# Clustered attention: the row of maxima copied directly, two int64 staging buffers, and new slots for every preparation step

## The chip, the cores and the metric

One Trainium2 chip, one of its cores. The metric is device time in microseconds of one execution; lower is better. The core has five engines that run side by side, each in the order of its own program: TensorE (PE in the rows; PEld is its weight load), VectorE (DVE), ScalarE (ACT), GpSimd (POOL), and SyncE (SP), whose sequencer issues all the transfers of this kernel.

## What is computed

Clustered attention, followed by two mixture layers whose code the change does not touch. With 4 batches, 8 heads, 768 positions and a head dimension of 64:

```python
q_assign = np.argmax(np.einsum('bhsd,hcd->bhsc', q_n, c_n), axis=-1)
k_assign = np.argmax(np.einsum('bhsd,hcd->bhsc', k_n, c_n), axis=-1)
mask = q_assign[:, :, :, None] == k_assign[:, :, None, :]
scores = scale * np.matmul(q, k.transpose(0, 1, 3, 2))
scores = np.where(mask, scores, -1000000000.0)
scores = scores - np.max(scores, axis=-1, keepdims=True)
attn = np.exp(scores)
attn = attn / (np.sum(attn, axis=-1, keepdims=True) + 1e-09)
return np.matmul(attn, v).astype(np.float32)
```

The result goes through `g = h * cos(h)` with `h = x @ w_in`, where `w_in` and `w_out` are 64-bit floats that the kernel receives as int64 and converts itself, and then through a soft mixture of eight experts.

## The kernel before

The attention works on 16 pairs of heads. For each pair there is a stack `st` in SBUF (three of them, used in turn), with the high and low parts of q and k, 32 rows that encode the cluster mask, and on partition 96 one row that holds, for each query, its maximum with the sign turned. The score matmuls (L399, L400) read this stack, so that the maximum is subtracted by the matmul itself, and ScalarE's exponential (L403) needs no bias. A pair has 12 units `u`: two chunks of 384 queries by six tiles of 128 keys, with a score for each of the two heads. After every second unit the matmuls with v follow (`av`, tile `o`, L412), and GpSimd adds up the exponentials (`ps`, L417 and L420).

While pair j is scored, the next pairs are made ready. For pair j+1 there are 24 maxima matmuls (`smax`, tile `sm`, L364), each emptied by a reduction of VectorE (`mc`, L366). `smax_fin` gathers the maxima of one chunk, and `smax_row` turns them by a transpose (L379) into a tile `mrow` of 6 partitions by 128 (L381) and brings them to partition 96 of the stack. For pair j+2 q and k are transposed (`prep_T`), split into high and low parts (`prep_hi`, `prep_lo`: qlo and klo on VectorE, L275) and copied to the stack; `prep_cl`, `prep_ct`, `prep_mx`, `prep_eq`, `prep_eqt`, `prep_mask` and `prep_rows` make the mask rows. Beside that two blocks of 128 by 512 weights are converted per pair: `conv_load` fetches the int64 words into the tile `w64`, `conv_do` has eight steps (0, 1, 3, 4, 5 and 6 on VectorE, 2 and 7 on ScalarE). In this text cvo0 to cvo7 are the steps of the first block of a pair (w_out), cvi0 to cvi7 those of the second (w_in).

The order of all this is written out by hand in the tables `POS` and `FIRST` (L521 to L544). A pair has 48 slots, four to a unit: before the first score, between the scores, after the second score, and after `av`. `at4(g, q, f)` puts a step into slot q of the pair that begins at unit g. `FIRST` holds the slots of the first pair, which runs with less prepared. The program is emitted in that order, so the slot of a step sets its place on every engine. Transfers that need an engine's result are put off by a number of slots (`defer`, `tick`), and SyncE issues them in that order; a transfer that has to wait holds all the later ones.

Nearly all matmuls of the preparation share three PSUM banks in turn (`mbank`), so a matmul can start only when the bank that was used three matmuls earlier has been emptied.

The row of maxima goes to partition 96 in two transfers, through a DRAM tile:

```python
defer(DL, out=mds[i, qc], in_=mrow.bitcast(F32))
defer(DL + 6, out=st[96:97, Q1:Q1 + 2, QW * qc:QW * qc + QW].bitcast(F32),
      in_=mds[i, qc].rearrange("(o h t) p -> o h (t p)", h=2, o=1))
```

Of the kernel before, what the change touches and what calls it, by code (L numbers as in the profile page):

```python
# [8 lines left out]
F32 = mybir.dt.float32  # L9
F32R = mybir.dt.float32r  # L10
BF16 = mybir.dt.bfloat16
I32 = mybir.dt.int32
# [7 lines left out]
P = 128  # L20
# [6 lines left out]
def clustered_attention_then_soft_moe(  # L27
# [20 lines left out]
    NPAIR = B * NP  # L48
    KT = S // P
    QW = S // 2  # L50
# [10 lines left out]
    dram = ctx.enter_context(tc.tile_pool(name="dram", bufs=1, space=DRAM))  # L61
# [6 lines left out]
    def mbank(nm, shape=(P, 512), dt=F32):  # L68
        mcnt[0] += 1
        return psum.tile(list(shape), dt, tag=f"m{mcnt[0] % ring[0]}", name=nm)  # L70
# [8 lines left out]
    mask = const.tile([P, 2], F32, name="mask")  # L79
    vm = const.tile([P, NPAIR], F32, name="vm")  # L80
# [4 lines left out]
    sums = [dram.tile([H, S], F32, name=f"sums{b}") for b in range(B)]  # L85
    recs = [dram.tile([H, S], F32, name=f"recs{b}") for b in range(B)]
    wod = dram.tile([DF, DM], F32, name="wod")
    mds = {(i, c): dram.tile([6, P], F32, name=f"mds{i}_{c}") for i in range(NPAIR) for c in range(2)}

    wc = [wbig.tile([P, 2, DT, 512], F32R, tag="wbig", name=f"wc{f}") for f in range(NF)]  # L90

# [58 lines left out]
    with ExitStack() as a:  # L150
        at_p = a.enter_context(tc.tile_pool(name="at", bufs=3))
        two = a.enter_context(tc.tile_pool(name="a2", bufs=2))
# [4 lines left out]
        Q1, Q2, K1, K2 = 0, 2, 4, 6  # L157
        T = {}
        late = []
        DL = 3  # L160

        def defer(n, **kw):
            late.append([n, kw])
# [212 lines left out]
        def smax_row(i, qc):  # L376
            s, st = T[i], stacks[i % 3]
            g = mbank(f"mrow{i}_{qc}")
            PE.transpose(g[0:6, 0:P], s["m6", qc], ident)  # L379
            mrow = two.tile([6, P], F32R, tag="mrow", name=f"mrow_{i}_{qc}", bufs=1)  # L380
            DVE.tensor_scalar(out=mrow, in0=g[0:6, 0:P], scalar1=-BIG / 2, scalar2=-1.0, op0=ALU.max, op1=ALU.mult)  # L381
            defer(DL, out=mds[i, qc], in_=mrow.bitcast(F32))
            defer(DL + 6, out=st[96:97, Q1:Q1 + 2, QW * qc:QW * qc + QW].bitcast(F32),
                  in_=mds[i, qc].rearrange("(o h t) p -> o h (t p)", h=2, o=1))

        def smax_rowpe(i, qc):
            s, st = T[i], stacks[i % 3]
# [59 lines left out]

        def conv_load(n):
            w, r, c = conv[n]
            st = two.tile([P, 1024], I32, tag="w64", name=f"w64_{n}", bufs=1)  # L450
            src = w_in if w == "i" else w_out
            SP.dma_start(out=st, in_=src[r * P:(r + 1) * P, c * 512:(c + 1) * 512].bitcast(I32))
            T["c", n] = st
# [61 lines left out]
        def at(g, pos, f, *args):  # L515
            fill.setdefault((g, pos), []).append((f, args))

        def at4(g, q, f, *args):
            at(g + q // 4, q % 4, f, *args)

        POS = {  # L521
            "T": [3, 7, 0, 1, 7, 12, 17, 23],
            "c": [12, 16],
            "m": [16, 20, 25, 28],
            "rows": [42, 35, 42, 36],
            "ld": 16,
            "cv": [[4, 4, 4, 8, 9, 12, 16, 17], [28, 29, 30, 35, 37, 42, 42, 45]],
            "wp": [23, 34, 40],
            "sm": [0, 5, 6, 7, 10, 10, 15, 17, 18, 26, 26, 27, 20, 21, 21, 32, 34, 36, 36, 40, 41, 43, 45, 46],
            "fin": [1, 4, 30, 35],  # L530
            "vm": [6, 28, 19],
        }
        FIRST = {
            "eqt": 7,
            "mask": 8,
            "rows": [9, 12, 12, 10],
            "cv": [3, 6, 8, 11, 15],
            "ld": 9,
            "wp": [21, 26, 36],
            "sm0": [2, 2, 5, 5, 6, 7, 8, 12, 15],  # L540
            "sm1": [13, 15, 16, 21, 22, 24, 24, 25, 26, 26, 28, 29, 17, 29, 31, 33, 34, 38, 40, 41, 42, 42, 44, 45],
            "fin0": [15, 19],
            "fin1": [33, 35],
        }  # L544

        def place_conv(n, g):
            pos = POS["cv"][n % 2]
            for k, x in enumerate(pos):
                at4(g, x, conv_do, n, k)
            if n + 1 < len(conv):  # L550
                at(g + pos[5] // 4 + 1, 0, conv_load, n + 1)
            if conv[n][0] == "o":
                r = conv[n][1]
                for x, f in zip(POS["wp"], (wphi_T, wphi_mm, wphi_sum)):
                    at4(g, x, f, r)

        for n in range(1, len(conv)):
            place_conv(n, 12 * (n // 2))
# [42 lines left out]
        for j in range(NPAIR):  # L601
            g = 12 * j
            f = POS["fin"]
            if j:
                at(g - 8, 0, load_v, j)
                at4(g, f[0], smax_fin, j, 1, True)
                at4(g, f[1], smax_row, j, 1)
            if j > 1:
                at4(g - 12, f[2], smax_fin, j, 0, True)
                at4(g - 12, f[3], smax_row, j, 0)  # L610
            at4(g, POS["vm"][0], prep_vm, j)
            at4(g, POS["vm"][1], prep_vm2, j)
            if j < NPAIR - 1:
                at4(g + 12, POS["vm"][2], sumq, j)
            if j % NP == NP - 1 and j < NPAIR - 1:
                at(g + 20, 2, recip0, j // NP)
                at(g + 23, 3, recip, j // NP)
# [19 lines left out]
        def flush():  # L637
            while late:
                tick()

        conv_load(0)
        ACT.activation(out=cn, in_=cn, func=AF.Exp, scale=-1.0)
        consts2()
# [46 lines left out]
        for x in range(3, 8):  # L690
            at4(0, FIRST["cv"][x - 3], conv_do, 0, x)
        at4(0, FIRST["ld"], conv_load, 1)
        for x, f in zip(FIRST["wp"], (wphi_T, wphi_mm, wphi_sum)):
            at4(0, x, f, 0)
        pend = []
        for g in range(GE):
            i, u = divmod(g, NU)
# [58 lines left out]
    with ExitStack() as m:  # L756
# [299 lines left out]
        for h in range(2):  # L1056
            x = slice(256 * h, 256 * h + 256)
            DVE.scalar_tensor_tensor(out=acc[:, x], in0=acc[:, x], scalar=cr, in1=ap[h], op0=ALU.mult, op1=ALU.add)
            g = psum.tile([P, 512], F32, tag="s", name=f"acct{h}", bufs=3)[:, 0:256]
# [164 lines left out]
```

## Time and profile before

| | us |
|---|---|
| runs of the kernel | 957.63, 959.75, 960.16 |
| median | 959.75 |
| profiled execution | 960.29 |
| its span, first to last instruction | 958.4 |
| mean granted clock of TensorE | 0.989 |

The page has the busy time of each engine, the idle time before groups of instructions and what ended it, and the chain of work that ended last. A matmul's end is modelled: consecutive score matmuls start 0.18 us apart, though each is shown with 0.34 us. So what a wait costs is best read from the starts, and the idle time that the trace gives is about 0.16 us less. A stretch from about 32 to 503 us is the attention; the two mixture layers follow.

### The profile page before, as it was taken

To read this page: it belongs to the slowest core of one execution; us is meant where nothing else is said; L and a number is where in the kernel's file an instruction comes from. 1 tells how busy PE (TensorE), PEld (TensorE's weight loads), DVE (VectorE), ACT (ScalarE), POOL (GpSimd) and SP (SyncE) were. 2 spreads that over 40 slices of the span, in tenths; PEclk is the share of its full clock that TensorE was granted. 3 is DMA by queue.
4 is the path that set the end of the run, shared out by engine and by line. 5 is a ranking of instruction groups with operands and counts; after the bars stand their busy time and mean duration, and the time that the engine had idled before them with its cause. 6 is when DMAs were issued, how large, how long until landed. Compare 5 with 4: busy or idle time off the path is not lost.

```text
span 958.4 us, 16925 instructions
## 1 busy us (share of the span) xinstructions
PE 904.9 (94%) x5994; PEld 622.8 (65%) x5994; DVE 716.2 (75%) x1459; ACT 674.5 (70%) x1420; POOL 459.3 (48%) x342
## 2 busy tenths in 40 slices
PE   5798999999999999999999999999999999999995
PEld 3465666666666666656656777777777777677543
DVE  6778888988888888879786777777777777775402
ACT  4657888777887778867664677767776777676423
POOL 3437877788777878776862222222222222220000
PEclk9889999999999999999999999999999999999998
DMA  8966667776668766676231043304331111117899
GB/s 173 211 149 157 162 175 196 192 197 155 166 176 213 191 172 166 174 186 166 89 95 54 24 132 117 125 25 132 119 123 36 33 37 31 45 26 295 333 360 326
DMA packets 132515, 142.18 MB, mean 148 GB/s; under 512 B 58408, under 2 KB 105808, under 8 KB 132432
## 3 DMA queue, kind: packets, MB, share of 16 engines
q1 hardware_dynamic: 132432, 141.11, 53.2%
q8 instruction: 47, 0.77, 0.3%
q14 instruction: 36, 0.29, 0.1%
HBM read 86.27 MB, written 17.06 MB: 108 GB/s over the span
## 4 chain that ended last, share of the span: by engine, by line
PE 68%; DVE 11%; ACT 9%; DMA 7%; issue 2%; SPq 2%; POOL 0%; ACTq 0%; POOLq 0%
PE h L138 21%; PE o L412 12%; PE sm L364 6%; PE s L399 6%; PE s L400 5%; PE gt L784 3%; DVE mc L366 3%; DMA mds<-mrow 3%; PE lp L810 2%; PE accp L893 2%; DVE qlo L275 2%; ACT L772 2%; DMA st<-mds 2%; PE he L1101 1%; ACT L848 1%
## 5 line engine op out<-in xcount | busy, mean ns | idle before, releaser
L138 PE MATMUL h<-wc,xhi 128*128 128x512 f32 x768 | 249.6, 406 | 6.7 <-DVE gg L777 6.5
L420 POOL TENSOR_TENSOR ps<-ps,a 128x768 f32<-128x768 f32 x120 | 235.3, 1961 | 37.9 <-ACT a L403 18.2
L366 DVE TENSOR_REDUCE mc<-sm 128x1 f32<-128x384 f32 x384 | 199.1, 547 | 30.3 <-PE sm L364 27.9
L403 ACT ACTIVATE a<-s 128x384 f32<-128x384 f32 x384 | 175.8, 491 | 26.2 <-PE s L400 20.4
L138 PEld LDWEIGHTS h<-wc,xhi 128*128 128x128 f32 x768 | 137.3, 189 | 56.9 <-DVE kk L147 15.9
L138 PE MATMUL h<-wc,xlo 128*128 128x512 f32 x384 | 151.7, 395 | 0.0
L399 PE MATMUL s<-st 97*128 97x384 f32 x384 | 141.8, 369 | 7.3 <-DMA st<-mds 6.9
L412 PE MATMUL o<-a,vt 128*64 128x384 f32 x768 | 147.7, 506 | 0.0
L364 PE MATMUL sm<-st 96*128 96x384 f32 x384 | 135.8, 385 | 10.1 <-DVE mc L366 6.1
L400 PE MATMUL s<-st 128*128 128x384 f32 x384 | 130.5, 340 | 0.0
L364 PEld LDWEIGHTS sm<-st 96*128 96x128 f32 x384 | 72.4, 194 | 50.4 <-DVE mc L366 17.5
L777 DVE SCALAR_TENSOR_TENSOR gg<-kk,h 128x512 f32<-128x512 f32 x96 | 66.0, 687 | 50.6 <-ACT kk L774 47.8
L772 ACT ACTIVATE kk<-kk 128x512 f32<-128x512 f32 x96 | 60.6, 631 | 42.0 <-DVE kk L147 41.7
L399 PEld LDWEIGHTS s<-st 97*128 97x128 f32 x384 | 73.1, 190 | 23.1 <-issue 11.1
L412 PEld LDWEIGHTS o<-a,vt 128*64 128x64 f32 x768 | 47.2, 137 | 57.6 <-issue 57.3
L109 POOL TENSOR_TENSOR xn<-xn,rc 128x512 f32<-128x512 f32 x24 | 31.3, 1304 | 109.0 <-DMA rc<-recs 109.0
L138 PEld LDWEIGHTS h<-wc,xlo 128*128 128x128 f32 x384 | 72.2, 188 | 17.0
L400 PEld LDWEIGHTS s<-st 128*128 128x128 f32 x384 | 73.4, 191 | 0.0
L417 POOL TENSOR_TENSOR ps<-a,a 128x768 f32<-128x768 f32 x30 | 54.8, 1827 | 37.5 <-ACT a L403 33.7
L113 POOL TENSOR_TENSOR xn<-xn,rc 128x512 f32<-128x512 f32 x24 | 32.0, 1332 | 84.0 <-DVE rc L111 78.9
L121 POOL TENSOR_TENSOR xlo<-xn,xhi 128x512 fp32r<-128x512 f32 x24 | 36.5, 1522 | 67.5 <-DVE xhi L120 66.0
L147 DVE SCALAR_TENSOR_TENSOR kk<-kk,h 128x512 f32<-128x512 f32 x96 | 66.0, 688 | 3.3
(218 smaller groups left out, 1530.0 us busy)
## 6 DMA issues: line engine op xcount, KB each, us to landing
w<-in_moe_w_dram SPq DMA_DIRECT2D x8, 2048.0 KB
wh<-in_moe_w_dram SPq DMA_DIRECT2D x26, 512.0 KB
st<-qhi SPq DMA_DIRECT2D x32, 384.0 KB
st<-khi SPq DMA_DIRECT2D x64, 192.0 KB
w<-in_moe_w_out_dram SPq DMA_DIRECT2D x16, 512.0 KB
w<-in_moe_w_in_dram SPq DMA_DIRECT2D x16, 512.0 KB
qt<-in_q_dram SPq DMA_DIRECT2D x32, 192.0 KB
kt<-in_k_dram SPq DMA_DIRECT2D x32, 192.0 KB
```

Of the source, the lines that this page charges most:

```text
L138: PE.matmul(h, lhsT=x[:, d, :], rhs=wc[f][:, w, d, :], start=(n == 0), stop=(n == 3 * DT - 1))
L147: DVE.scalar_tensor_tensor(out=a, in0=a, scalar=-TWO_PI, in1=h, op0=ALU.mult, op1=ALU.add)
L364: PE.matmul(m[:, 0:QW], lhsT=st[0:96, Q1 + h, qt * P:(qt + 1) * P], rhs=st[0:96, K1 + h, half * QW:(half + 1) * QW], start=True, stop=True)
L366: DVE.tensor_reduce(out=s["mc"][:, col:col + 1], in_=m[:, 0:QW], op=ALU.max, axis=AX.X)
L399: PE.matmul(x[:, 0:QW], lhsT=st[0:97, K1 + h, ks], rhs=st[0:97, Q1 + h, qs], start=True, stop=False)
L400: PE.matmul(x[:, 0:QW], lhsT=st[:, K2 + h, ks], rhs=st[:, Q2 + h, qs], start=False, stop=True)
L403: ACT.activation(out=T[i][u][:, h, :], in_=x[:, 0:QW], func=AF.Exp, scale=scale)
L412: PE.matmul(s["o"][64 * h:64 * h + 64, 0:QW], lhsT=s["v"][:, h, kt, :], rhs=t[:, h, :], start=(kt == 0), stop=(kt == KT - 1))
L417: (DVE if i == NPAIR - 1 else POOL).tensor_tensor(out=ps, in0=s[u - 1], in1=t, op=ALU.add)
L420: (DVE if i == NPAIR - 1 else POOL).tensor_tensor(out=ps, in0=ps, in1=t, op=ALU.add)
L772: ACT.activation(out=r, in_=r, func=AF.Sin, scale=0.5)
L777: DVE.scalar_tensor_tensor(out=R["g", t][:, f * 512:(f + 1) * 512], in0=r, scalar=0.5, in1=h, op0=ALU.subtract, op1=ALU.mult)
```

## The change

The row of maxima goes from `mrow` straight to partition 96, in two transfers of three partitions each, one for each head, and the DRAM tiles `mds` are gone. The staging tile `w64` gets two buffers instead of one, and the load of the next block has slots of its own (`cl`) instead of following step 5 of the block before. All the numbers of `POS` and `FIRST` but a few are new.

```diff
-    mds = {(i, c): dram.tile([6, P], F32, name=f"mds{i}_{c}") for i in range(NPAIR) for c in range(2)}
...
-            defer(DL, out=mds[i, qc], in_=mrow.bitcast(F32))
-            defer(DL + 6, out=st[96:97, Q1:Q1 + 2, QW * qc:QW * qc + QW].bitcast(F32),
-                  in_=mds[i, qc].rearrange("(o h t) p -> o h (t p)", h=2, o=1))
+            for h in range(2):
+                defer(DL, out=st[96:97, Q1 + h, QW * qc:QW * qc + QW].bitcast(F32).rearrange("o (t p) -> o t p", p=P),
+                      in_=mrow[3 * h:3 * h + 3].bitcast(F32))
...
-            st = two.tile([P, 1024], I32, tag="w64", name=f"w64_{n}", bufs=1)
+            st = two.tile([P, 1024], I32, tag="w64", name=f"w64_{n}")
...
-            "rows": [42, 35, 42, 36],
+            "rows": [35, 35, 38, 43],
...
-            "fin": [1, 4, 30, 35],
-            "vm": [6, 28, 19],
+            "fin": [3, 6, 34, 36],
+            "vm": [24, 30, 11],
+            "cl": [1, 41],
...
-                at(g + pos[5] // 4 + 1, 0, conv_load, n + 1)
+                at4(g, POS["cl"][n % 2], conv_load, n + 1)
```

On SyncE, the transfers at the end of a pair: before, the row goes to DRAM and comes back (the second waits for the landing of the first, DMAHW6), and the load of the next int64 block waits for VectorE and ScalarE to have read the buffer. The names in brackets are the counters that an instruction waits for.

```order
L170 DMA st_153<-klo_1432 64x768 [waits DMAHW3_49,DVE_49]
L170 DMA st_153<-klo_1432 64x768 [waits DMAHW4_49]
L170 DMA xnum_81<-num_0_1463 128x384 [waits DMAHW5_49,Activation_49]
L170 DMA mds_0_100<-mrow_0_1526 6x128 [waits DMAHW6_49,DVE_49]
L170 DMA st_152<-mds_0_100 1x2x384 [waits DMAHW7_49,DMAHW6_49]
L452 DMA w_6_1581<-in_moe_w_out_dram 128x1024 [waits DMAHW0_49,DVE_49,Activation_49]
```

The same place with the change:

```order
L169 DMA xnum_81<-num_0_1044 128x384 [waits DMAHW2_49,Activation_49]
L169 DMA st_120<-klo_1046 64x768 [waits DMAHW3_49,DVE_49]
L169 DMA st_120<-klo_1046 64x768 [waits DMAHW4_49]
L169 DMA st_122<-mrow_0_1119 1x3x128 [waits DMAHW5_49,DVE_49]
L169 DMA st_122<-mrow_0_1119 1x3x128 [waits DMAHW6_49]
L451 DMA w_4_1152<-in_moe_w_out_dram 128x1024 [waits DMAHW7_49]
```

Two transfers of half a row have taken the place of the two hops, and each waits for the row on VectorE but for no landing of the other hop.

On VectorE, from the fifth step of the first conversion block to the first maxima of the second half, before (qlo is the low part of q; t and val belong to the conversion):

```order
L476 SCALAR_TENSOR_TENSOR t_4_1257<-w_4_1198,t_4_1257 128x512
L275 TENSOR_TENSOR qlo_1326<-qT_1251,qhi_1294 128x768
L366 TENSOR_REDUCE mc_1223<-sm_6_1347 128x1
L478 TENSOR_TENSOR val_1258<-val_1258,t_4_1257 128x512
L307 TENSOR_REDUCE amx_1359<-e_1357 128x24
L366 TENSOR_REDUCE mc_1223<-sm_7_1376 128x1
L366 TENSOR_REDUCE mc_1223<-sm_8_1383 128x1
```

With the change, from the two maxima of slot 10 to sm_15:

```order
L365 TENSOR_REDUCE mc_1191<-sm_2_1277 128x1
L365 TENSOR_REDUCE mc_1191<-sm_13_1280 128x1
L473 TENSOR_SCALAR t_4_1217<-w_4_1152 128x512
L274 TENSOR_TENSOR qlo_1307<-qT_1220,qhi_1270 128x768
L365 TENSOR_REDUCE mc_1191<-sm_14_1314 128x1
L475 SCALAR_TENSOR_TENSOR t_4_1217<-w_4_1152,t_4_1217 128x512
L365 TENSOR_REDUCE mc_1191<-sm_3_1323 128x1
L477 TENSOR_TENSOR val_1218<-val_1218,t_4_1217 128x512
L365 TENSOR_REDUCE mc_1191<-sm_4_1344 128x1
L306 TENSOR_REDUCE amx_1359<-e_1333 128x24
L311 TENSOR_TENSOR eq_1363<-e_1333,amx_1359 128x384
L365 TENSOR_REDUCE mc_1191<-sm_5_1370 128x1
```

The conversion's steps 5 and 6 have moved behind qlo, and eq ahead of sm_5.

On TensorE, the end of that stretch with the change (s are scores, wt the transposes of a converted block):

```order
L398 MATMUL s_5_0_1365<-st_122 128x384
L399 MATMUL s_5_0_1365<-st_122 128x384
L363 MATMUL sm_5_1370<-st_120 128x384
L398 MATMUL s_5_1_1373<-st_122 128x384
L399 MATMUL s_5_1_1373<-st_122 128x384
L363 MATMUL sm_6_1377<-st_120 128x384
L489 MATMUL wt_1380<-ident,val_1218 128x128 x4
L363 MATMUL sm_15_1387<-st_120 128x384
```

The maxima sm_5, sm_6 and the transposes wt take the three banks, and sm_15 is the next to need sm_5's; before, sm_12 to sm_14 stood at this place.

## Rows read from the trace of the kernel before

**Rows 1.** Busy time by stretch: length, then each engine, granted clock, DMA share.

```profile
99.00:128.00 29.00, 28.24 (x174) 18.18 (x174) 25.39 (x45) 23.28 (x52) 22.94 (x17) 1.00 0.70 182
```

**Rows 2.** Timeline of TensorE, first scores of pairs 1 and 13: start, duration, work.

```profile
74.26 0.34 PE L399 MATMUL s<-st 97*128 97x384 f32 x1
...
427.32 0.45 PE L399 MATMUL s<-st 97*128 97x384 f32 x1 [1.81 <-DMA st<-mds]
```

**Rows 3.** Waits of the whole span: total us, times, longest.

```profile
DVE t L466 <- DMA w<-in_moe_w_out_dram: 28.3, 14, 3.7
...
PEld s L399 <- DMA st<-mds: 9.9, 12, 2.1
...
PE sm L364 <- DVE mc L366: 6.1, 9, 1.5
```

**Rows 4.** Chain of waits, 244 to 252 us, and the matmul before its last piece.

```profile
244.36 0.28 DVE mrow L381
...
244.84 4.29 DMA mds<-mrow
...
249.14 1.82 DMA st<-mds
...
249.71 0.41 PE L364 MATMUL sm<-st 96*128 96x384 f32 x1
251.01 0.44 PE L399 MATMUL s<-st 97*128 97x384 f32 x1 [0.89 <-DMA st<-mds]
```

**Rows 5.** Chain of waits: eight o matmuls behind 427 us, and eight usual ones.

```profile
428.77 2.76 PE o L412 x8
434.92 1.44 PE o L412 x8
```

**Rows 6.** Timeline of TensorE, 231 to 235 us.

```profile
231.16 0.34 PE L400 MATMUL s<-st 128*128 128x384 f32 x1
232.22 0.44 PE L364 MATMUL sm<-st 96*128 96x384 f32 x1 [0.72 <-DVE mc L366]
...
234.03 0.85 PE L432 MATMUL sum<-ps,ones 128*32 128x384 f32 x8
```

**Rows 7.** Timeline of TensorE: the waits in the first pair and at its end.

```profile
44.81 0.45 PE L364 MATMUL sm<-st 96*128 96x384 f32 x1 [1.52 <-DVE mc L366]
...
73.98 0.44 PE L364 MATMUL sm<-st 96*128 96x384 f32 x1 [1.45 <-ACT st L335]
```

**Rows 8.** Timeline of VectorE: qlo and eq without and with a neighbour.

```profile
47.73 0.94 DVE L275 TENSOR_TENSOR qlo<-qT,qhi 128x768 fp32r<-128x768 f32 x1
...
56.34 0.55 DVE L312 TENSOR_TENSOR eq<-e,amx 128x384 bf16<-128x384 f32 x1
...
229.27 2.43 DVE L275 TENSOR_TENSOR qlo<-qT,qhi 128x768 fp32r<-128x768 f32 x1
...
234.07 1.62 DVE L312 TENSOR_TENSOR eq<-e,amx 128x384 bf16<-128x384 f32 x1
```

**Rows 9.** Timeline of GpSimd: the addition that runs when the second qlo starts.

```profile
229.05 1.83 POOL L417 TENSOR_TENSOR ps<-a,a 128x768 f32<-128x768 f32 x1
```

**Rows 10.** Timeline of TensorE: first and last matmul of a stretch in pair 7.

```profile
256.50 0.51 PE L364 MATMUL sm<-st 96*128 96x384 f32 x2
...
265.78 0.42 PE L399 MATMUL s<-st 97*128 97x384 f32 x1
```

**Rows 11.** Groups of VectorE: busy, mean ns of one, idle before.

```profile
L366 DVE TENSOR_REDUCE mc<-sm 128x1 f32<-128x384 f32 x384 | 199.1, 547 | 30.3 <-PE sm L364 27.9
L275 DVE TENSOR_TENSOR qlo<-qT,qhi 128x768 fp32r<-128x768 f32 x15 | 27.3, 1818 | 0.2 <-ACT qhi L258 0.2
L312 DVE TENSOR_TENSOR eq<-e,amx 128x384 bf16<-128x384 f32 x16 | 22.9, 1429 | 0.1
L472 DVE SCALAR_TENSOR_TENSOR val<-val,t 128x512 f32<-128x512 f32 x32 | 21.7, 677 | 0.0
```

**Rows 12.** Busy time and granted clock (after POOL) by stretch in the first pair.

```profile
46.00:54.00 8.00, 7.43 (x32) 3.74 (x29) 3.60 (x5) 2.08 (x5) 3.13 (x2) 0.57 1.09 232
```

More of the change, by code (lines that the diff above doesn't have):

```diff
@@ L521, in clustered_attention_then_soft_moe @@
         POS = {
-            "T": [3, 7, 0, 1, 7, 12, 17, 23],
-            "c": [12, 16],
-            "m": [16, 20, 25, 28],
-            "rows": [42, 35, 42, 36],
[L526 to L529, printed above, removed]
-            "fin": [1, 4, 30, 35],
-            "vm": [6, 28, 19],
+            "T": [3, 8, 0, 3, 9, 12, 16, 28],
+            "c": [11, 15],
+            "m": [19, 20, 26, 28],
+            "rows": [35, 35, 38, 43],
+            "ld": 8,
+            "cv": [[3, 5, 5, 10, 11, 14, 15, 23], [29, 29, 29, 36, 39, 42, 43, 45]],
+            "wp": [23, 29, 41],
+            "sm": [0, 6, 10, 14, 17, 21, 22, 25, 26, 26, 28, 34, 1, 10, 13, 24, 33, 34, 36, 37, 38, 40, 44, 44],
+            "fin": [3, 6, 34, 36],
+            "vm": [24, 30, 11],
+            "cl": [1, 41],
         }
         FIRST = {
[L534 to L543, printed above, removed]
+            "eqt": 2,
+            "mask": 2,
+            "rows": [12, 10, 9, 10],
+            "cv": [0, 2, 7, 13, 23],
+            "ld": 11,
+            "wp": [25, 27, 44],
+            "sm0": [0, 1, 3, 5, 7, 7, 10, 16, 19],
+            "sm1": [12, 14, 14, 16, 19, 21, 23, 23, 29, 30, 31, 34, 18, 20, 21, 26, 27, 33, 38, 40, 42, 42, 42, 44],
+            "fin0": [19, 21],
+            "fin1": [36, 38],
         }
```

## The prediction

> **What bounds the kernel now.** I read the page first, then the busy time by stretch, the waits, the chain around one pair's start, and the timelines of TensorE, VectorE and GpSimd there. The profiled execution took 960.29 us, its span 958.4. The change touches the attention stage alone, from about 32 to 503 us. There TensorE is busy for 28.2 of 29 us in an undisturbed stretch, while VectorE has 25.4, ScalarE 23.3 and GpSimd 22.9 [rows 1]. So TensorE sets the pace, and a change here is worth what it takes from TensorE's idle time, no more. What is idle shows in the pairs' starts: pair 1 starts at 74.26 us and pair 13 at 427.32 [rows 2], so twelve pairs take 353.1 us, 29.4 each. The two waits that are costed below take 9.9 and 5.5 us of them, 1.3 a pair, so about 28.1 is the floor that the matmuls and the small waits set. The prize over twelve pairs is some 15 us, and a little more in the first pair and the thirteenth.
>
> The waits name it [rows 3]. TensorE's weight loads wait 9.9 us in 12 places for st<-mds, which is the row of maxima coming back from DRAM. Its matmuls wait 6.1 us in 9 places for a reduction of VectorE (L366), which must empty one of three PSUM banks. VectorE in turn stands 28.3 us in 14 places waiting for the int64 weights w. The last is no loss by itself: VectorE is not the bound and these waits lie at a pair's opening, where few reductions are due.
>
> **The row of maxima.** In the chain from 244 to 251 us the row is computed at 244.36, the copy to DRAM is issued at 244.84 and takes 4.29 us, the copy back takes 1.82 more, and the first score matmul of the next pair starts at 251.01 [rows 4]. The matmul before it stands at 249.71, so without the wait it would have started at 249.97 and 1.04 us were lost. The change drops the first copy and issues two copies of half a row instead, so the count of transfers stays at four per pair and SyncE's queue gets no longer. It also stops holding SyncE until the first copy has landed. The row is now made one slot later and behind one more reduction of 0.5 us, so it is ready about 4.7 us before the pair's start, where it was 5.3. What one direct copy of 1.5 KB takes, no row shows. The nearest short one is the copy back, 1.82 us. The long one of the same chain is the copy to DRAM, 4.29. The first copy was issued 0.2 us after the row, and I allow 0.5 for issuing two (an estimate); the second half then lands 2.5 or 5.0 us after the row. I take the short value: in the old order the copy to DRAM stands right behind klo's two copies and num's, with khi's four shortly before; in the new one khi's four stand 19 slots ahead of the row, klo's two 8 slots ahead, and the load of w behind it. So the wait goes: **-9.9 us**. With the long value 0.3 us at 14 starts would come back, +4.2. The other row of a pair, due in the middle, is issued behind the new load of q and k but has 15 slots until it is needed, about 8.8 us at 0.585 us a slot (28.1 over 48), so I cost that move at nothing.
>
> One start cost more. At 427.32 TensorE had been idle for 1.81 us by the gap column, and the eight o matmuls behind it took 2.76 us where eight normally take 1.44 [rows 2, 5]. If that wait goes, so does the slow stretch: **-1.3 us**.
>
> **The reduction that frees a bank.** At 232.22 a maximum matmul (L364) starts 1.06 us after its predecessor at 231.16, where 0.18 is usual [rows 6]; 0.88 is lost, of which the gap column shows 0.72. The 6.1 us in 9 places [rows 3] hold 1.52 from the opening [rows 7] and a short one of 0.2; what is left is 4.4 in seven pairs, with 0.16 more each 5.5. The cause stands on VectorE: qlo took 2.43 us in this pair and 0.94 where GpSimd had nothing to do [rows 8]. In the slow case a ps addition of GpSimd of 1.83 us had begun 0.22 us earlier [rows 9], and qlo ended 0.82 us after that addition. The late bank was that of sm_6, whose reduction stood right behind qlo. In the new order sm_14 stands there, and its bank is wanted again by sm_4 after much the same matmuls. But one conversion step of 0.68 now stands behind qlo instead of ahead of it [rows 11], and the sums, 0.85 on TensorE [rows 6], come before sm_14 instead of behind: about 1.5 us more room where 0.88 were lost. **-5.5 us** from the old place.
>
> The same price has to be asked of the new order. The tight place there is sm_15, which needs the bank that the reduction of sm_5 frees. From the two maxima in slot 10 to sm_15 TensorE runs two groups of o, six scores, cl, the sums, ct, wt and seven maxima. The same set with one more maximum lies between 256.50 and 265.78 in a pair without that stall [rows 10]: 9.28 us, so 9.1. VectorE must do in it three steps of the conversion at 0.68, six reductions at 0.52 (busy time by count), amx, a reduction like them, qlo and eq [rows 11]. Without the last two that is 5.7 us, and the first reduction starts when its matmul of 0.44 ends [rows 6], so 6.1. With the means 1.82 and 1.43 it is 9.4, which exceeds 9.1 by 0.3. With 0.94 and 0.55, the unhindered values [rows 8], nothing is lost; with 2.43 and 1.62 it is 10.2 and 1.1 are lost. I take the mean, since GpSimd is as full as before: 13 pairs by 0.3, **+4 us** (0 to +14.3).
>
> The Trainium skill (SBUF — State Buffer, "Who interferes with whom") says that a VectorE instruction with two SBUF inputs and a GpSimd instruction that reads SBUF exclude each other for the whole instruction. By that rule the worst qlo would be 0.94 + 1.83 = 2.8 us and the top of this term about 19 instead of 14.3; the trace agrees with the order of things, its longest being 2.5.
>
> **The second staging buffer.** It takes away the 28.3 us of VectorE. I cost it at nothing on TensorE's path, as said, though it is why VectorE enters the tight stretch without backlog. If its load came late after all, VectorE would again stand 2 us there (28.3 in 14 places), with the same small effect as now. The five additions of prep_vm move from slot 6 to 24 on GpSimd and their reader vm2 from 28 to 30; GpSimd has 6 us free in 29 [rows 1], so I cost this at nothing.
>
> **The prepared mask rows.** At 73.98 the first maximum of the next pair waits 1.45 us for ScalarE's st rows (L335) [rows 7]. In the table two of the four row steps move from slot 42 to 35 and 38, and the one that the first maximum needs is done by 39 even in the pair that runs four slots late: **-1.6 us**.
>
> **The opening (first pair).** Before, TensorE waits 1.52 us at 44.81, and the granted clock is 0.57 of full speed from 46 to 54 us [rows 7, 12], most of it at the lower of the two levels (1.2 of 2.4 GHz); 8 us at 0.43 less are 3.4 us of work lost. The new first table puts all four row steps of VectorE at one place, earlier, and the maxima of pair 1 right behind ScalarE's last row step. It can lose all of the 4.9 or add another wait like the 1.45. I take 0 (-4.9 to +1.5).
>
> Sum: -9.9 - 1.3 - 5.5 + 4 - 1.6 = -14.3, so 946.0 for the profiled execution's 960.29. Its time stands 0.5 above the median of the runs, 959.75, so the forecast is **945.5 us**. About 0.3% (2.9 us) is what a measurement of this kernel can tell from no change. The later stages (the h matmuls and the tail) are untouched and move along.
>
> **Rivals.**
> 1. VectorE becomes the bound: qlo and eq both fall behind a GpSimd addition in every pair, 1.1 at sm_15. For it: 25.4 of 29 us busy, and eq now stands right ahead of the reduction that frees sm_15's bank. Against: VectorE no longer loses 2 us to w. With +14.3 for +4: 955.8; with an opening 1.5 worse, 957.3.
> 2. The direct copies land late. Price as if one took what both did, 6.1 us: the second half would be ready 6.8 after the row is made, 2.1 late at 14 starts, 29.4 in place of 9.9, and the slow stretch stays. 959.75 + 19.5 - 5.5 + 4 - 1.6 = 976.2, slower. It decides from 0.9 us late per start, that is from 5 us from issue to landing. For it: a copy from three partitions into one stands in no row. Against: the copy back also writes one partition, in 1.82.
> 3. The change does not remove the bank stall, only shifts it: -5.5 falls away, 951.0.
>
> **How the numbers follow.** Forecast 0.64 (939 to 950), rival 3 0.12 (950 to 953), rival 1 0.17 (953 to 960), rival 2 0.07. The range from 938 to 957 leaves out rival 2, the upper part of rival 1 and a better opening together with no stall. Faster by over 0.3% (under 956.9): the forecast, rival 3 and a little under half of rival 1, 0.84. Within: the rest of rival 1, 0.09. Slower: rival 2, 0.07.
>
> **What would show it.** The first score of each pair starts within 0.3 us of the matmul before it, and no wait for st<-mrow is left. Pairs 1 to 12 take 28.3 to 28.5 us. VectorE no longer waits for w. sm_15 shows 0.3 us of idle in most pairs. Wrong would be a wait for st<-mrow, a pair of 29 us or more, or a granted clock below full after the opening.

## The result and the profile after

| | before | after |
|---|---|---|
| median, us (runs) | 959.95 (4) | 935.52 (4) |
| range of the runs | 957.63 to 961.21 | 934.97 to 937.5 |
| ratio, 95% interval | | 0.9743 [0.9713, 0.9773] |
| span of the profiled execution | 958.4 | 933.3 |

The change makes the kernel 24.4 us faster, 2.6%. The forecast was 945.5 with a range from 938 to 957: the direction was right, the gain was 10 us larger than forecast and the time lies below the range.

The line numbers of the direct copies' kernels are one lower (L398 for the first score matmul, L363 for the maxima). Busy time by stretch, changed kernel, with the columns of [rows 1] and [rows 12]:

```profile
99.00:128.00 29.00, 29.00 (x183) 19.38 (x183) 24.68 (x47) 24.86 (x56) 23.93 (x17) 1.00 0.72 199
46.00:54.00 8.00, 7.71 (x45) 5.17 (x46) 5.66 (x13) 4.16 (x10) 6.84 (x8) 1.00 1.08 213
```

TensorE is now busy for the whole of the 29 us, where it was for 28.24 [rows 1], and the granted clock from 46 to 54 us, in the first pair, is 1.00 where it was 0.57 [rows 12]. Timeline of TensorE, the first scores of pairs 1, 5 and 13, with the matmul ahead of the last two:

```profile
69.83 0.35 PE L398 MATMUL s<-st 97*128 97x384 f32 x1
...
181.69 0.42 PE L363 MATMUL sm<-st 96*128 96x384 f32 x1
181.95 0.34 PE L398 MATMUL s<-st 97*128 97x384 f32 x1
...
403.31 0.42 PE L363 MATMUL sm<-st 96*128 96x384 f32 x1
403.56 0.34 PE L398 MATMUL s<-st 97*128 97x384 f32 x1
```

Pairs 1 to 12 take 333.7 us, 27.8 each, where they took 353.1 [rows 2]; pairs 2 to 12 are all alike, at 27.70. The first score starts 0.25 or 0.26 us behind its predecessor, which is the usual interval at this place. The row's own timeline before pair 5, VectorE and SyncE:

```profile
177.12 0.27 DVE L380 TENSOR_SCALAR mrow<-mrow 6x128 fp32r<-6x128 f32 x1
...
177.42 1.50 SPq L169 DMA_DIRECT2D st<-mrow  x2
```

Both copies are issued at once, the second 0.8 us behind the first, and the row has 4.55 us from its end to the score. That is all the time in which the two copies had to land, and no first score of any pair waited. Of the waits of [rows 3], the one for st<-mds and its like for st<-mrow have gone from the list, and VectorE's for w is left in one place of 14; of the 6.1 us for a reduction 0.3 are left. Waits from 30 to 500 us:

```profile
DVE t L465 <- DMA w<-in_moe_w_out_dram: 1.2, 1, 1.2
```

By starts of first scores in the two profiled executions, the span's 25.1 us come from here:

| stretch | before | after | difference |
|---|---|---|---|
| up to the first score | 32.4 | 33.8 | +1.4 |
| pair 0 | 41.9 | 36.0 | -5.9 |
| pair 1 | 29.9 | 29.0 | -0.9 |
| pairs 2 to 12 | 323.1 | 304.7 | -18.4 |
| pair 13 | 30.1 | 27.4 | -2.7 |
| pair 14 | 24.9 | 24.8 | -0.1 |
| pair 15 and what follows | 476.1 | 477.6 | +1.5 |

The difference in the last line can't be told from chance: that stretch takes 473 to 479 us in the kernels below, old or new slots.

### The profile page after: what moved, and what is told of

It reads as the page before. It is cut to its first block, busy times and chain, and to the rows that moved or that the text cites. A ratio compares the mean times of both kernels' runs of the same rounds, so it can differ in the third digit from the quotient of the medians.

```text
span 933.3 us, 16978 instructions
## 1 busy us (share of the span) xinstructions
PE 892.4 (96%) x5994; PEld 624.1 (67%) x5994; DVE 694.0 (74%) x1459; ACT 674.7 (72%) x1420; POOL 462.1 (50%) x342
## 4 chain that ended last, share of the span: by engine, by line
PE 79%; ACT 9%; DVE 6%; DMA 2%; SPq 1%; issue 1%; POOL 0%; ACTq 0%; POOLq 0%
PE h L137 20%; PE o L411 15%; PE s L398 9%; PE sm L363 8%; PE s L399 7%; PE gt L784 3%; PE lp L810 2%; PE accp L893 2%; ACT L772 2%; ACT L848 2%; PE he L1101 2%; ACT kk L772 1%; DVE gg L777 1%; PE tpq L248 1%; PE tpk L248 1%; PE sum L431 1%
## 5 line engine op out<-in xcount | busy, mean ns | idle before, releaser
L365 DVE TENSOR_REDUCE mc<-sm 128x1 f32<-128x384 f32 x384 | 204.0, 553 | 70.7 <-PE sm L363 67.9
L402 ACT ACTIVATE a<-s 128x384 f32<-128x384 f32 x384 | 180.1, 493 | 29.6 <-PE s L399 26.5
L411 PE MATMUL o<-a,vt 128*64 128x384 f32 x768 | 145.1, 499 | 0.0
L398 PE MATMUL s<-st 97*128 97x384 f32 x384 | 143.7, 374 | 0.0
L363 PE MATMUL sm<-st 96*128 96x384 f32 x384 | 131.3, 376 | 3.2 <-DVE st L336 2.1
L363 PEld LDWEIGHTS sm<-st 96*128 96x128 f32 x384 | 72.1, 195 | 29.5 <-DVE t L475 8.4
L398 PEld LDWEIGHTS s<-st 97*128 97x128 f32 x384 | 72.9, 190 | 27.1 <-issue 25.1
L772 ACT ACTIVATE kk<-kk 128x512 f32<-128x512 f32 x96 | 60.6, 631 | 41.9 <-DVE kk L146 41.5
```

The costliest lines, as they stand in the source:

```text
L363: PE.matmul(m[:, 0:QW], lhsT=st[0:96, Q1 + h, qt * P:(qt + 1) * P], rhs=st[0:96, K1 + h, half * QW:(half + 1) * QW], start=True, stop=True)
L365: DVE.tensor_reduce(out=s["mc"][:, col:col + 1], in_=m[:, 0:QW], op=ALU.max, axis=AX.X)
L398: PE.matmul(x[:, 0:QW], lhsT=st[0:97, K1 + h, ks], rhs=st[0:97, Q1 + h, qs], start=True, stop=False)
L402: ACT.activation(out=T[i][u][:, h, :], in_=x[:, 0:QW], func=AF.Exp, scale=scale)
L411: PE.matmul(s["o"][64 * h:64 * h + 64, 0:QW], lhsT=s["v"][:, h, kt, :], rhs=t[:, h, :], start=(kt == 0), stop=(kt == KT - 1))
L772: ACT.activation(out=r, in_=r, func=AF.Sin, scale=0.5)
```

## The experiments

Eight kernels make up a full table of the change's three parts: the row by two direct copies or through DRAM (hop), one or two staging buffers, old or new slots. With two buffers the load of w stands at its new slots 1 and 41, with one at its old place behind step 5. Medians in us (before stood at 959.2 to 959.6 beside these runs):

| | old slots, one buffer | old, two | new slots, one buffer | new, two |
|---|---|---|---|---|
| hop | 959.6 (before) | 947.0 | 984.5 | 946.5 |
| direct | 944.4 | 938.6 | 953.5 | 935.5 (after) |

No part's worth stands by itself: the direct copies give 8 to 31 us, the second buffer with its load 6 to 38, and the new slots anything from +25 to -3. (A median of four runs is good to about 3 us here, by the intervals below.) Why that is so is what the runs are read for.

### The direct copies alone (direct_only)

```diff
-            defer(DL, out=mds[i, qc], in_=mrow.bitcast(F32))
...
+            for h in range(2):
+                defer(DL, out=st[96:97, Q1 + h, QW * qc:QW * qc + QW].bitcast(F32).rearrange("o (t p) -> o t p", p=P),
+                      in_=mrow[3 * h:3 * h + 3].bitcast(F32))
```

> The kernel before with the direct copies alone. Theory (each removed wait is worth what it cost): the row lands 2.5 us after it is made, the 9.9 us of waits for st<-mds and the slow stretch behind 427 us go, about 949. Rival (the stall moves): the wait at a pair's start had given VectorE time, so the wait of sm_8 for its bank now shows in every pair at up to 0.9 us instead of in seven; 5 us come back, about 954.

Measured: 944.4 us, ratio 0.9847 [0.982, 0.9873]. Pairs 2 to 12 take 27.8 us each, with the old slots, old buffer and old order on VectorE. The stall at sm_8 has gone too, and neither expectation had that. From the timeline of VectorE and GpSimd in pair 5:

```profile
197.55 0.68 DVE L475 SCALAR_TENSOR_TENSOR t<-w,t 128x512 f32<-128x512 uint32 x1
198.15 0.95 DVE L274 TENSOR_TENSOR qlo<-qT,qhi 128x768 fp32r<-128x768 f32 x1
198.19 2.61 POOL L416 TENSOR_TENSOR ps<-a,a 128x768 f32<-128x768 f32 x1
```

qlo starts 0.04 us ahead of the ps addition. In pairs 2 to 12 it is 0.04 to 0.05 us ahead, but for pair 10, where the two start together. It takes 0.95 in all of them, and now ps is the long one, 2.61 where it took 1.83 [rows 9].

### Two buffers alone (buffers_only): what a late row costs

```diff
-            st = two.tile([P, 1024], I32, tag="w64", name=f"w64_{n}", bufs=1)
+            st = two.tile([P, 1024], I32, tag="w64", name=f"w64_{n}")
...
-                at(g + pos[5] // 4 + 1, 0, conv_load, n + 1)
+                at4(g, POS["cl"][n % 2], conv_load, n + 1)
```

> The kernel before with two staging buffers and load slots 1 and 41 alone; hop and old slots kept. Beside direct copies the second buffer gave 5.8 us (944.4 to 938.6). Theory (it serves the first pair and the last pairs, where other waits do not cover it, and is independent of the hop): 953 to 957 us, VectorE's 28.3 us of waits for w gone, the score waits for st<-mds still about 10 us. Rival (it helps only once the row is in time): 958 to 961 us. Third: the w load no longer stands far ahead of the read-back, the hop gets later, over 962 us.

Measured: 947.0 us, 0.9869 [0.9848, 0.9891]. None of the three expectations held: two buffers help the hop itself. The waits of the weight loads for the row were 9.9 us in 12 places [rows 3]; from 30 to 500 us they are now

```profile
PEld s L399 <- DMA st<-mds: 1.5, 4, 0.5
```

This run shows more, since some of its pairs start on time and some a little late. Pair 5, late by 0.09 us, and pair 6, on time (TensorE, VectorE, GpSimd):

```profile
188.85 0.44 PE L399 MATMUL s<-st 97*128 97x384 f32 x1
...
197.00 1.83 POOL L417 TENSOR_TENSOR ps<-a,a 128x768 f32<-128x768 f32 x1
...
197.16 2.48 DVE L275 TENSOR_TENSOR qlo<-qT,qhi 128x768 fp32r<-128x768 f32 x1
...
200.17 0.44 PE L364 MATMUL sm<-st 96*128 96x384 f32 x1 [0.78 <-DVE mc L366]
...
226.11 0.95 DVE L275 TENSOR_TENSOR qlo<-qT,qhi 128x768 fp32r<-128x768 f32 x1
226.15 2.61 POOL L417 TENSOR_TENSOR ps<-a,a 128x768 f32<-128x768 f32 x1
```

In pair 6 qlo is 0.04 us ahead of ps. In pair 5 TensorE's late start moved the reductions ahead of qlo, so qlo came 0.16 us behind ps; it ended 0.81 us after ps did, and the bank stall followed. For each pair the table gives the row's lateness (start of the first score less that of the matmul before it, less the usual 0.25), the duration of qlo, and how much longer the pair's 174 matmuls took, interval by interval, than the same matmuls in pair 5 of direct_only:

| pair | before: late, qlo, longer | buffers_only: late, qlo, longer | qlo_first: late, qlo, longer |
|---|---|---|---|
| 2 | 0.13, 2.47, 1.35 | 0, 0.95, 0.01 | 1.75, 2.15, 4.19 |
| 3 | 0.16, 2.44, 1.41 | 0, 0.95, 0.01 | 0.18, 1.25, 0.91 |
| 4 | 0.24, 2.09, 1.38 | 0, 0.95, 0.02 | 1.13, 2.05, 1.82 |
| 5 | 0.44, 2.14, 1.37 | 0.09, 2.48, 1.35 | 0.80, 1.36, 1.92 |
| 6 | 0.07, 2.43, 1.37 | 0, 0.95, 0.01 | 0.68, 2.49, 1.88 |
| 7 | 1.05, 1.54, 1.35 | 0, 0.95, 0.00 | 0.16, 1.23, 0.88 |
| 8 | 1.07, 1.53, 1.35 | 0.45, 2.13, 1.35 | 0.68, 2.49, 1.90 |
| 9 | 1.60, 0.95, 1.73 | 0, 0.95, 0.01 | 0.94, 2.24, 1.83 |
| 10 | 1.14, 1.44, 1.37 | 0.17, 2.42, 1.39 | 0.15, 1.24, 0.92 |
| 11 | 0.75, 1.84, 1.41 | 0, 0.95, 0.01 | 0.64, 2.54, 1.88 |
| 12 | 0.17, 2.40, 1.37 | 0, 0.95, 0.01 | 0, 0.98, 0.02 |

In the first two columns a pair loses nothing or 1.35 to 1.4, whether its row is late by 0.07 us or by 1.14; only the one late by 1.60 loses more. The row's lateness and the bank stall are one loss, whose size is set by ps. GpSimd's ps starts 8.25 us after the time at which the pair could have started, in every pair, for GpSimd then works on what it has from earlier; it doesn't move with the row. On time, qlo starts at 8.20. Late, it starts behind ps and ends at 10.9, however late it was. TensorE pays about 1.05 us by then, as lateness or as stall, and 0.30 more in intervals of 0.05 to 0.11: behind the first score, behind sm_8, at wt. Their cause stays open.

A late row is not the only thing that makes qlo late. In the kernel before, VectorE works without a break of more than 0.15 us from the arrival of w to qlo in each of pairs 2 to 12, so there w, and not the row, sets when qlo starts: 5.9 to 6.2 us after w, which comes 2.5 to 3.8 us after the time at which the pair could have started. In buffers_only VectorE never waits for w, and the late row alone does it. Pair 6 of the kernel before (its qlo is in [rows 8]), and pair 13 of direct_only, where the row is on time and w is late (VectorE, GpSimd):

```profile
223.35 0.69 DVE L466 TENSOR_SCALAR t<-w 128x512 int32<-128x512 int32 x1 [1.74 <-DMA w<-in_moe_w_out_dram]
```

```profile
415.38 0.69 DVE L465 TENSOR_SCALAR t<-w 128x512 int32<-128x512 int32 x1 [1.72 <-DMA w<-in_moe_w_out_dram]
...
420.66 1.83 POOL L416 TENSOR_TENSOR ps<-a,a 128x768 f32<-128x768 f32 x1
421.30 2.01 DVE L274 TENSOR_TENSOR qlo<-qT,qhi 128x768 fp32r<-128x768 f32 x1
```

That pair takes 1.37 us more than the same pair in old_tables below, where VectorE does not wait for w. In pairs 2 to 12 of direct_only VectorE waits 0.5 to 0.9 us for w, and nothing is lost. Row and w are late together in the kernel before because SyncE issues the load of w 0.11 us behind the read-back, in every one of these pairs, and the read-back waits for the first hop. The direct copies free both: VectorE's 28.3 us of waits for w [rows 3] are 10.0 in direct_only.

The Trainium skill (SBUF — State Buffer, "Who interferes with whom") says that it is the order of issue that decides who blocks. The trace agrees: the same two instructions take 0.95 and 2.61 us in one order, 2.48 and 1.83 in the other.

### qlo ahead of a conversion step (qlo_first, buffers_qlo_first)

If that race decides, then qlo asked for earlier must move the point from which a late row loses it. One number of the old table, in the kernel before and in buffers_only:

```diff
-            "cv": [[4, 4, 4, 8, 9, 12, 16, 17], [28, 29, 30, 35, 37, 42, 42, 45]],
+            "cv": [[4, 4, 4, 8, 9, 13, 16, 17], [28, 29, 30, 35, 37, 42, 42, 45]],
```

> The kernel before with one number changed: step 5 of the first conversion block from slot 12 to 13, so that VectorE does qlo ahead of it and asks for it 0.68 us sooner, about 7.5 us after the time at which the pair could have started. Theory (late row and bank stall are one loss: a row that is late by 0.07 us or more puts qlo behind GpSimd's ps addition, which starts 8.25 us after that time; qlo then ends at 10.9 however late the row was, and the pair is 1.35 us longer, of which the row's lateness is a part): pairs whose row is late by less than 0.5 now take 27.8 plus the lateness plus at most 0.4, with qlo under 1.3 us; pairs late by over 0.8 still lose the race, have a conversion step of 0.68 behind qlo's end, and take 29.3 to 30.0. Time 950 to 959 us. Rival (late row and bank stall are two losses that the order on VectorE does not tie together): every pair stays 1.3 to 1.4 us above 27.8 with the split of before, 958 to 961 us.

Measured: 958.7 us, 0.9984 [0.9958, 1.001], no change by time; the pairs tell (last column of the table). A row late by 0.15 to 0.18 no longer puts qlo behind ps, and these pairs lose 0.9 instead of 1.4; that is more than the theory allowed, and 0.38 of it is one wait ahead of vm. Rows late by 0.64 or more lose the race and take 1.8 to 1.9, again whatever the lateness; the pair of 1.75 had other waits beside. In this execution seven rows were so late, against five in the kernel before, and gain and loss cancel. Pairs 3 and 6 of qlo_first, timeline of VectorE and GpSimd:

```profile
144.59 1.25 DVE L275 TENSOR_TENSOR qlo<-qT,qhi 128x768 fp32r<-128x768 f32 x1
144.98 2.57 POOL L417 TENSOR_TENSOR ps<-a,a 128x768 f32<-128x768 f32 x1
...
233.01 1.82 POOL L417 TENSOR_TENSOR ps<-a,a 128x768 f32<-128x768 f32 x1
233.16 2.49 DVE L275 TENSOR_TENSOR qlo<-qT,qhi 128x768 fp32r<-128x768 f32 x1
```

> The kernel with two staging buffers alone (947.0 us; in three of eleven pairs the row was late by 0.09, 0.17 and 0.45 us, and just these took 1.35 us more), with the same step of the conversion behind qlo. Theory: no pair with qlo over 1.3 us, every pair within 27.8 to 28.4, 942 to 945 us. Rival (the 1.35 us follows from the late row itself): late pairs still cost 1.35, 946 to 948 us.

Measured: 946.5 us, 0.9838 [0.9802, 0.9873], against 947.0 without it. The theory missed; the time is in the rival's range, but its 1.35 us for a late row is not there. Three rows were late by 0.60 to 0.71 us this time, lost the race and cost 1.82 to 1.88; the one late by 0.30 kept qlo at 1.08 and cost 0.88. The mechanism is as above; how late a row comes is not set by this edit.

### The load left at its place (buffer_old_load)

```diff
-            st = two.tile([P, 1024], I32, tag="w64", name=f"w64_{n}", bufs=1)
+            st = two.tile([P, 1024], I32, tag="w64", name=f"w64_{n}")
```

> The kernel before with two staging buffers, the load of w left at its old place in SyncE's queue (behind step 5, ahead of the loads of q and k). Two buffers with the loads at slots 1 and 41 gave 12.2 us. Theory (the place does it: the load of 512 KB ahead of q, k and v makes all the transfers up to the row later, and its wait for the conversion is short): 955 to 961 us, rows still issued 0.3 to 3 us late. Rival (the wait for the one buffer does it): 944 to 949 us, rows issued at once.

Measured: 960.2 us, 1.0006 [0.9982, 1.003]; the theory holds. The second buffer alone gives nothing in the kernel before; the 12.2 us of buffers_only need the new place of the load in SyncE's queue. (The new place with one buffer was not run.) SyncE's queue in the middle of pair 6, kernel before and, behind it, buffers_only:

```profile
232.92 0.60 SPq L452 DMA_DIRECT2D w<-in_moe_w_in_dram  x1
233.62 1.99 SPq L178 DMA_DIRECT2D qt<-in_q_dram  x2
235.65 2.53 SPq L178 DMA_DIRECT2D kt<-in_k_dram  x2
```

```profile
229.19 2.22 SPq L178 DMA_DIRECT2D qt<-in_q_dram  x2
231.46 1.34 SPq L178 DMA_DIRECT2D kt<-in_k_dram  x2
```

With 512 KB of w ahead of q, k and v, SyncE comes later to everything up to the row. Over the rows of pairs 2 to 13, the read-back is issued 4.1 us after the row is made in the kernel before, 4.0 in buffer_old_load, and 2.9 in buffers_only, where SyncE has caught up in time to issue the first hop within 0.2 us in ten of twelve. The load at the pair's start also stays behind the read-back in buffer_old_load, and VectorE still waits 26.2 us in 12 places for w. In its pair 6 the row was on time and w late (a wait of 1.57 us): qlo took 2.59, and the pair was 1.37 us longer.

### Direct copies and two buffers, old tables (old_tables)

Both of the edits above in the kernel before:

```diff
-            defer(DL, out=mds[i, qc], in_=mrow.bitcast(F32))
...
-            st = two.tile([P, 1024], I32, tag="w64", name=f"w64_{n}", bufs=1)
+            st = two.tile([P, 1024], I32, tag="w64", name=f"w64_{n}")
...
+            "cl": [1, 41],
```

> The changed kernel with both tables of slots as they were (direct copies, two staging buffers and their load slots stay). Theory: the second buffer is worth nothing on TensorE's path, so this is as the direct copies alone, within 1 us. Rival (VectorE's backlog comes from its waits for w): the stall of sm_8 goes too, 5 us below the direct copies alone.

Measured: 938.6 us, 0.9789 [0.9759, 0.982], 5.8 less than direct_only. Both missed: the steady pairs stay at 27.81. By profiled spans it is 4.1: 1.4 in pair 13, which takes 27.39 instead of 28.76, 1.4 in pair 0, and the rest behind the attention. The part in pair 13 is shown: it is the late w of direct_only above, and with two buffers VectorE does not wait for w at all. The others are not; pair 0 takes 41.9 to 47.3 us in the seven kernels with the old tables, and what follows pair 14 varies as said.

### The new slots without the direct copy, or with one buffer

In slots_only the changed kernel gets both back:

```diff
+            defer(DL, out=mds[i, qc], in_=mrow.bitcast(F32))
...
+            st = two.tile([P, 1024], I32, tag="w64", name=f"w64_{n}", bufs=1)
...
+                at(g + pos[5] // 4 + 1, 0, conv_load, n + 1)
```

> The changed kernel with the row of maxima through DRAM as before and one staging buffer, so the new slots alone. Theory (waits add up): 935.5 + 9.9 + 1.3 = 947, with st<-mds waits of 0.8 us a pair. Rival (the slots do nearly everything): in the new order the hop to DRAM is no longer behind khi and klo, takes 1.5 and the way back 1.8, and the waits for st<-mds shrink to under 0.3 a pair: under 940.

Measured: 984.5 us, 1.0259 [1.0221, 1.0298]: slower than before, and both were wrong. Timeline of SyncE and first scores of pair 5 and of its second half:

```profile
190.83 0.35 SPq L452 DMA_DIRECT2D w<-in_moe_w_out_dram  x1
191.27 0.62 SPq L170 DMA_DIRECT2D st<-mds  x1
...
194.54 0.41 PE L399 MATMUL s<-st 97*128 97x384 f32 x1 [1.69 <-DMA st<-mds]
...
199.25 1.32 SPq L178 DMA_DIRECT2D qt<-in_q_dram  x2
200.63 1.33 SPq L178 DMA_DIRECT2D kt<-in_k_dram  x2
202.06 0.48 SPq L170 DMA_DIRECT2D mds<-mrow  x1
...
205.74 1.33 SPq L170 DMA_DIRECT2D st<-mds  x1
...
209.23 0.42 PE L399 MATMUL s<-st 97*128 97x384 f32 x1 [0.28 <-DMA st<-mds]
```

Two places are late. At the pair's start the load of w stands ahead of the read-back and waits for the conversion to free the one buffer (SyncE's own waits, 100 to 420 us):

```profile
SPq L452 <- DVE t L476: 23.3, 10, 2.4
```

The first score is 1.7 to 2.1 us late in all but one of pairs 2 to 13. In the middle the first hop stands behind the new load of q and k, which the new table puts there. Each was then put back alone, the first line of that edit in slots_with_hop, the other two in slots_one_buffer.

> The changed kernel with the row of maxima again sent through DRAM; two staging buffers, new slots. The new slots with hop and one buffer took 984.5 us, with 29.1 us of score waits for st<-mds in 23 places; this run tells which of the two old parts does it. Theory (the hop does it: the row is made some 4.5 us before its use and its second transfer waits for the landing of the first): 960 to 980 us, 20 us or more of waits for st<-mds, pairs of 29.3 to 30.7 us. Rival (the one buffer does it: the load of w waits for the conversion and holds the read-back of the row behind it in SyncE's queue): under 945 us, waits for st<-mds under 5 us, pairs of 27.7 to 28.

Measured: 946.5 us, 0.9869 [0.9838, 0.9899]. The time is just above the rival's: pairs 2 to 12 take 27.9 to 29.2 us. All starts but two are late by under 0.3 us, so the one buffer made those; the middle rows are still up to 1.1 late, and that is the hop's 11 us against after. No qlo is over 1.23 here: with the new slots it comes in the last half us of ps, and a pair loses 0.1 to 0.5 us more than its two rows are late.

> The changed kernel with one staging buffer again and its load behind step 5 of the block before; direct copies, new slots. Theory (the hop alone made the new slots slow, and a late load costs VectorE time only where few reductions are due): 936 to 943 us, pairs of 27.7 to 28.1, VectorE waits again for w for 10 us or more in total. Rival (the one buffer holds SyncE's queue): 955 us or more, with score waits for st<-mrow.

Measured: 953.5 us, 0.9929 [0.99, 0.9959]. Neither: no score waits for the row, yet pairs take 27.7 to 31.3. Waits, and ScalarE and TensorE at 208 us:

```profile
ACT val L469 <- DMA w<-in_moe_w_in_dram: 15.5, 11, 2.1
PE sm L363 <- ACT vm L351: 11.9, 11, 1.8
```

```profile
208.87 0.66 ACT L469 ACTIVATE val<-w 128x512 f32<-128x512 f32 x1 [1.63 <-DMA w<-in_moe_w_in_dram]
...
209.80 0.17 ACT L351 ACTIVATE vm<-vm 128x1 f32<-128x1 f32 x1
...
210.02 0.44 PE L363 MATMUL sm<-st 96*128 96x384 f32 x1 [1.30 <-ACT vm L351]
```

The load comes late, ScalarE's conversion step (L469) waits for it at the head of its queue, the copy vm behind that step empties a PSUM bank, and TensorE waits for the bank. (Whether two buffers with the load at this old place would do the same was not run.) Step 2 is on ScalarE; the prediction and this expectation looked at VectorE alone.

### The slots of the vs additions (vm_back)

```diff
-            "vm": [24, 30, 11],
+            "vm": [6, 28, 11],
```

> The changed kernel with prep_vm and its reader at their old slots 6 and 28, so that GpSimd's five short additions no longer run where eq runs. Theory (the forecast stall at sm_15 stays away because eq meets the short additions, 0.56 us, and not a ps addition of 1.8): eq takes 1.3 us or more in most pairs, sm_15 starts 0.2 to 1.0 us late, pairs of 27.9 to 28.7 instead of 27.70, 938 to 949 us. Rival (there is room anyway, since qlo takes 1.2 rather than 1.8): pairs stay at 27.70 within 0.05, 934 to 937 us.

Measured: 935.6 us, 0.9758 [0.9726, 0.9791]; the rival holds. Pairs 2 to 12 take 27.74, qlo 1.0, eq 0.56 again: eq now starts in the last 0.1 to 0.2 us of a ps. The short additions are not what keeps sm_15 free.

### The tables of the first pair (old_first, new_first)

The changed kernel with the whole old FIRST (old_first), and old_tables with the whole new one (new_first); one line of the former:

```diff
-            "sm0": [0, 1, 3, 5, 7, 7, 10, 16, 19],
+            "sm0": [2, 2, 5, 5, 6, 7, 8, 12, 15],
```

> The changed kernel with the old table for the first pair. Theory: only the opening changes; the wait at 44 us and the lower clock behind it are back, 4 to 6 us slower than the change, about 940, and every pair from the second on takes 27.7 us. Rival: the opening's gain comes from the second buffer or the later slots, and the time stays within 1 us of the change.

Measured: 940.4 us, 0.9812 [0.9782, 0.9842], 4.9 over after: steady pairs 27.70, pair 0 44.0 instead of 36.0. The time is as the theory had it, its reason is not: the wait of TensorE at 44 us is not there.

> Direct copies, two buffers and the new table of the first pair, with the old slots of all later pairs. Theory (with the row on time the new slots of the later pairs are worth 0.1 us a pair and no more, and the first table some 4.9): pairs 2 to 12 at 27.81, pair 0 at 36 to 38, 932 to 937 us. Rival (the new slots of the later pairs are needed for it): 939 us or more.

Measured: 940.1 us, 0.9775 [0.9739, 0.9811]; the rival holds. Steady pairs are at 27.81, but pair 0 takes 42.7. Timeline of TensorE in old_first and in new_first, then busy time by stretch in old_first, in new_first and in the changed kernel:

```profile
36.41 0.88 PE L248 MATMUL tpk<-ident,kt 128*128 128x128 f32 x3 [3.67 <-DMA kt<-in_k_dram]
```

```profile
46.31 0.45 PE L363 MATMUL sm<-st 96*128 96x384 f32 x1 [2.09 <-ACT st L334]
```

```profile
36.00:40.00 4.00, 3.59 (x15) 3.31 (x16) 1.46 (x3) 1.57 (x4) 0.19 (x1) 0.50 1.07 216
```

```profile
36.00:40.00 4.00, 3.66 (x16) 3.48 (x16) 1.11 (x2) 1.97 (x4) 0.00 (x0) 0.50 1.05 213
```

```profile
36.00:40.00 4.00, 3.22 (x19) 2.61 (x20) 3.07 (x6) 2.88 (x7) 0.77 (x1) 1.00 1.04 212
```

In old_first TensorE stands 3.7 us for k. In new_first it waits for the mask rows (L334) in two places, 3.7 us together. In the changed kernel neither wait is there. But the wait for k does not come from the table alone: k is used at 35.0 to 36.4 us in every kernel that waits for it, and how long TensorE has stood by then, 0.2 to 4.8 us, hangs on the table and on when its first score came; vm_back, with both new tables, waits 1.8. And the lower clock from 36 to 40 us, 0.50, is in both of these runs.

What holds over all runs is where pair 1 starts: at 67.9 to 69.9 us in the five kernels with both new tables, at 74.3 to 76.7 in the seven with both old ones, at 75.4 in old_first and 74.9 in new_first. So the gain needs the new FIRST and the new POS. From 34 to 56 us the clock is at its lower level for 6.8 to 13.6 us in those nine, and for none or 3.4 us in the five. Which of the old waits brings that about stays open.

## Why the prediction was wrong

1. **"The row of maxima", -9.9, "the slow stretch", -1.3, and "the reduction that frees a bank", -5.5.** The waits go as said, and the row is ready 4.55 us ahead where 4.7 was said. But they were costed as separate losses with separate cures, the bank by the new order on VectorE. direct_only shows one loss, cured with the old order once neither the row nor w is late. Together -16.7 was forecast; direct_only gives -18.5 in pairs 2 to 13 (353.2 to 334.7). The slow stretch was the clock, which the prediction did not name there. Busy time by stretch, kernel before, behind the start at 427.32:

```profile
428.00:432.00 4.00, 4.00 (x18) 1.59 (x16) 1.39 (x2) 1.65 (x4) 3.82 (x4) 0.57 0.27 101
```

   TensorE had stood 1.81 us, and was then granted the lower level for 3.4 us. In the changed kernel the clock is 1.00 from 70 to 456 us.
2. **"About 28.1 is the floor."** It is 27.81 with the old slots, 27.70 with the new. Subtracting the two waits from the period left 0.30 a pair that belongs to the same event and goes with it.
3. **"I take the mean ... +4 us" for sm_15.** This step failed outright: nothing was lost. The mean 1.82 of qlo was taken over pairs that met the ps addition near its start (2.5 us) or near its end (0.95), each by how late it was; it is the duration of no pair of the new order. With every pair alike qlo and eq take the same time in nearly every pair; from the changed kernel's timeline in pair 5, with sm_15 behind wt:

```profile
187.61 1.82 POOL L416 TENSOR_TENSOR ps<-a,a 128x768 f32<-128x768 f32 x1
...
189.02 1.23 DVE L274 TENSOR_TENSOR qlo<-qT,qhi 128x768 fp32r<-128x768 f32 x1
...
194.43 0.56 DVE L311 TENSOR_TENSOR eq<-e,amx 128x384 bf16<-128x384 f32 x1
...
195.51 0.60 PE L489 MATMUL wt<-ident,val 128*128 128x128 f32 x4
195.86 0.42 PE L363 MATMUL sm<-st 96*128 96x384 f32 x1
```

   The same sum with 1.23 and 0.56 is 6.1 + 1.8 = 7.9 us of VectorE in 9.1, with room. sm_15 starts without a wait. This and the point before make up some 8.5 of the missing 10 us (4, 0.3 in 11 pairs, 0.1 in 12); by starts, pairs 2 to 13 gave 21.1 where 12.7 was forecast.
4. **"The last is no loss by itself", and "the second staging buffer": nothing.** Both failed. VectorE's wait for w lies where VectorE has little to do, but in the kernel before it sets when qlo starts, and so the bank stall. And the buffer is not worth nothing: with its load at the new place 5.8 us beside direct copies and old slots, 18 beside the new ones, where ScalarE is held. With the old slots the buffer is worth what it lets the load do: move in SyncE's queue. That VectorE's waits would go was right: 28.3 us became 1.2.
5. **"The prepared mask rows", -1.6, and "the opening", 0.** The wait for the mask rows at 74 us is gone. All that lies before pair 2 gave 5.4 where 1.6 was forecast: the clock dip of [rows 12] did go, and the range of -4.9 to +1.5 held it. Its size in one execution is partly luck, as three other kernels with both new tables show 3.4 us at the lower level there.
6. **Rivals.** VectorE did not become the bound (24.7 of 29 us). The direct copies did not land late; the rival's mechanism shows in the hop with the new slots. The bank stall did not shift.

The range was too narrow below because the better opening and the missing stall were taken as exceptions; both came.

## What to carry to other kernels

When two stalls of a period add up to the same sum in every period, they are one loss with an anchor elsewhere: tabulate lateness, stall and total per period before adding them. A wait on an engine that is not the bound can be dear all the same: follow what it pushes back, here qlo 6 us later, before costing it at nothing. A duration that hangs on which of two instructions starts first has no mean to cost with; ask what sets the order, and whether the change fixes it. Slots written for one way of moving data can be worse than the old ones with another, so a load's place in the issuing queue is part of the price of what stands behind it.

## What the runs showed of the hardware

In buffers_only a lead of 0.04 us of qlo over a GpSimd addition, or a lag of 0.16, decides whether the pair costs 27.8 us or 1.35 more. The first hop of 3 KB took, at the starts of pairs 2 to 13 and from its issue to that of the read-back, 1.2 to 2.0 us in slots_with_hop and 1.6 to 4.4 in the kernel before [rows 4], the same transfer at two places of the queue. Issuing the two transfers of k took SyncE 2.9 us in the kernel before and 1.3 in buffers_only (medians from 100 to 420 us).
